# First block's queries and keys loaded in halves, four heads' bias tables behind them, matmuls over ones spread between the first quarters' scores

## The chip, the cores and the metric

The kernel runs on one core of a Trainium2 chip. The metric is device time in microseconds (us), taken over several executions; beside it one execution is recorded by the hardware profiler. The engines are named PE (TensorE; its weight loads are shown apart as PEld), DVE (VectorE), ACT (ScalarE), POOL (GpSimd) and SP (SyncE, which here only issues transfers).

## What is computed

Attention over 4 sequences of 576 tokens, 8 heads of 64, in a causal window of 128 with a linear position bias; a dense layer pair with h - tanh(h) between; and a layer of 8 experts in which each token goes to the one expert that fits it best.

```python
def _attn_ref(q, k, v):                      # 4 x 8 x 576 x 64 each
    scores = scale * np.matmul(q, k.transpose(0, 1, 3, 2))
    ...
    bias = slopes[:, None, None] * (-np.abs(rel).astype(np.float32))[None, :, :]
    mask = (rel >= 0) & (rel < window)       # window = 128
    scores = np.where(mask, scores + bias[None], -1000000000.0)
    attn = softmax(scores)
    return np.matmul(attn, v)

def _moe_ref(x, w_in, w_out):                # x 2304 x 512, w_in 512 x 2048
    h = x @ w_in
    return (h - np.tanh(h)) @ w_out

def _moe2_ref(x, expert_emb, tau, w1, w2):   # 8 experts of 512 x 1024 x 512
    logits = xn @ en.T / tau                 # of normalized rows
    expert_idx = np.argmax(logits, axis=1)
    ...
        out[mask] = gate_w[mask, None] * (np.maximum(x[mask] @ w1[e], 0.0) @ w2[e])
```

## The kernel before, in words

The 2304 tokens are 18 blocks of 128 rows, two blocks a group. A block's attention goes in four quarters of two heads each (function `quarter`): quarter number `a` is block `a // 4`, heads `2 * (a % 4)` and the next. For a quarter PE makes the scores (line 497 in the first four blocks, which work on plain float32 keys and queries), DVE adds the bias table and takes the maximum (line 525), ACT takes the exponentials (539), PE transposes them (560), ACT or DVE copies the transposes (564), and PE multiplies them with the values (574). Even quarters of the first two blocks write their scores to the bank "sc", odd ones to "acc". Per group, the rows are then transposed (678), multiplied with the weights of the dense layers (726, 750) and routed; the experts follow at the end.

The weights come as raw float32 and are split on the chip into a high and a low part: a load of 512 KB (line 347), a conversion on ACT or DVE (351), an assembly on DVE (354), the high part (359) and the low part (363). They are needed from about the third block on, so this work lies beside the attention of the first blocks.

Nothing of this is issued in the order of the source text. Every step is handed to a planner with `P.add(costs, function, due, r=..., w=...)`: which engines can do it and for how many us, when it is due, and which names it reads and writes. `Plan.order` takes, again and again, the step that can start first by these costs (the smaller due value where two can start at the same time), and so writes out one fixed order for each engine. SP's transfers share one assumed pipe in it. The order of all engines over the whole kernel comes from this one pass. The engines then run their queues in that order and wait for each other by semaphores.

At the start, `consts` loads the bias tables of the eight heads on ACT's queue, heads 0 and 1 first and heads 2 to 7 second, and then a mask `tri`, which the routing reads (line 876). SP loads queries and keys of the first block (`qk_early`, 256 KB each), a table of constants `con`, the values of the first block and then the other blocks' queries, keys and values and the raw weights. In the blocks 0 to 3 one transfer brings all eight heads of a block; its middle index is `hf * 2 + qq`, so the first two places are heads 0 to 3 (quarters 0 and 1) and the last two are heads 4 to 7.

`warm` puts matmuls over ones on PE, whose result nobody reads: `WARM[0]` of them at the very start, and `WARM[a + 1]` behind the scores of quarter `a`. Each is 128 x 128 by 512 columns in bf16. To the planner they read the bank of that quarter's scores, so that it places the softmax of the quarter behind them; on the chip they touch neither.

Of the kernel before, what the change touches and what calls it, by code (L numbers as in the profile page):

```python
# [23 lines left out]
B, H, S, D = 4, 8, 576, 64  # L24
# [23 lines left out]
WLEAD2 = 6  # L48
N0 = 1
NPX = 16  # L50
WARM = [7, 8, 2, 2, 2]
NALT = 8
NOWN = 8
NXO = 2
# [125 lines left out]
class Builder:  # L180
# [81 lines left out]

    def consts(self, P):
        nc, i = self.nc, self.i
        def table(e, h0, h1):
            nc.scalar.dma_start(out=self.bias[:, h0:h1, :],
                                in_=i["c_bias"][:, h0 * 256:h1 * 256].rearrange("p (h t) -> p h t", h=h1 - h0))

        for h0, h1 in ((0, 2), (2, H)):
            P.add({"AQ": 3.0}, lambda e, h0=h0, h1=h1: table(e, h0, h1), -40, w=[("bias", h) for h in range(h0, h1)])  # L270
        P.add({"AQ": 1.0}, lambda e: nc.scalar.dma_start(out=self.tri, in_=i["c_bias"][:, H * 256:]), -40, w=["tri"])

    def small(self):
        nc, i = self.nc, self.i
# [145 lines left out]
    def qk_early(self, P, b, due):  # L420

        nc, d2 = self.nc, b // 2

        def load_k(e):
            if b % 2 == 0:
                self.kf[d2] = self.wp.tile([128, 2, 4, 128], F32, tag=f"wo{FT - 1 - d2}", name=f"kf{d2}")
            nc.sync.dma_start(out=self.kf[d2][:, 1 - b % 2], in_=self.i["k0"][b])

        def load_q(e):
            if b % 2 == 0:  # L430
                self.qf[d2] = self.wp.tile([128, 2, 4, 128], F32, tag=f"w{'io'[d2]}{FT - 4}", name=f"qf{d2}")
            nc.sync.dma_start(out=self.qf[d2][:, b % 2], in_=self.i["q0"][b])

        both = lambda kind: [(kind, b)] + ([] if b % 2 else [(kind, b + 1)])
        P.add({"SP": 0.73}, load_q, -25 if b == 0 else due, r=["at"], w=both("qf"))
        P.add({"SP": 0.73}, load_k, -25 if b == 0 else due, r=["at"], w=both("kf"))

    def v_full(self, P, b, due):

# [29 lines left out]
    def quarter(self, P, a, due):  # L469

        nc = self.nc
        b, qd = divmod(a, 4)
        hf, qq = divmod(qd, 2)
        s, n = b % 2, (2 * b + hf) % 2
        one = b in NOPRE
# [8 lines left out]
        bank = "acc" if a < NALT and a % 2 else "sc"  # L484

        def scores(jj):
            sc = v["sc"][jj] = self.scores[jj] if bank == "sc" else self.psA.tile(
                [128, 2, 128], F32, tag=f"acc{jj}", name="scx", bufs=1)
            j = qq + 2 * jj
            hp, p0 = hf * 4 + j, 64 * jj  # L490
            if early:
                kt = [self.kf[x // 2][p0:p0 + 64, 1 - x % 2, hf * 2 + qq, :] for x in ([b] if one else [b, b - 1])]
                if b % 2 and not one:
                    kt = [self.kf[b // 2][p0:p0 + 64, :, hf * 2 + qq, :]]
                for m, k in enumerate(kt):
                    out = sc[:, 0:2, :] if b % 2 and not one else sc[:, m, :]
                    nc.tensor.matmul(out, lhsT=self.qf[b // 2][p0:p0 + 64, b % 2, hf * 2 + qq, :], rhs=k, start=True,  # L497
                                     stop=True)
                return
            q = self.qst[n]  # L500
            sl = s if one else slice(0, 2)
            for m in range(2):
                nc.tensor.matmul(sc[:, sl, :], lhsT=q[:, m, j, :], rhs=self.khl[:, sl, hp, :], start=(m == 0),  # L503
                                 stop=(m == 1))
# [118 lines left out]
        q = [("q", n), ("ql", n)]  # L623
        ttr = 0.4 if one else (0.52 if cs == 0 else 0.83)
        ttr += 0.13 * (2 * (b in SPLIT) + (b - 1 in SPLIT))
        for jj in range(2):
            if early:
                P.add({"PE": 0.3 if one else 0.42}, lambda e, jj=jj: scores(jj), due,
                      r=["at", ("qf", b)] + [("kf", x) for x in ([b] if one else [b, b - 1])], w=[(bank, jj)])
            else:  # L630
                P.add({"PE": 0.13 if one else 0.24}, lambda e, jj=jj: scores(jj), due,
                      r=["at"] + ks + [("kl", x, hf) for x in kv] + q, w=[(bank, jj)])
        if a + 1 < len(WARM) and WARM[a + 1]:
            self.warm(P, WARM[a + 1], -30, [(bank, 0), (bank, 1)])
        for jj in range(2):
            P.add({"DVE": ttr}, lambda e, jj=jj: soft(jj), due, r=["at", ("bias", qd * 2 + jj)],
                  w=[(bank, jj), ("mx", jj, a % 2)])
        for jj in range(2):
            P.add({"ACT": 0.49 if one else 0.64}, lambda e, jj=jj: exp(jj), due,
                  r=["at", (bank, jj), ("mx", jj, a % 2)], w=[("p32", pb, jj), ("sm", sk, qq, jj)])  # L640
        sm = [("sm", sk, x, y) for x in range(2) for y in range(2)]
        half = [("xr", 2 * hf), ("xr", 2 * hf + 1)]
        if early:
# [3 lines left out]
                  r=["at", ("tp", a)] + ([("h", own)] if own is not None else []), w=[("pt", a % 2)],  # L647
                  free="misc" if own is None else None)
            P.add({"PE": 0.45 if one else 0.9}, pv_f, due,
                  r=["at", ("pt", a % 2)] + [("vf", x) for x in ([b] if one else [b - 1, b])], w=[("o", qq)] if qq else ["o", ("o", 0), ("o", 1)])  # L650
            if qq:
# [4 lines left out]
              w=[("ph", a % 2)], port=True)  # L656
        P.add({"POOL": 0.84, "DVE": 0.46} if one else {"POOL": 1.19, "DVE": 0.71}, s_lo, due,
              r=["at", ("p32", pb, 0), ("p32", pb, 1), ("ph", a % 2)], w=[("ph", a % 2, 1)], port=True)
        P.add({"SP": 0.7 if one else 1.2}, tr, due, late=LATE, r=["at", ("ph", a % 2), ("ph", a % 2, 1)], w=[("pt", a % 2)])
        P.add({"PE": 0.28 if one else 0.56}, pv, due,  # L660
              r=["at", ("pt", a % 2)] + [("vt", x, hf, m) for x in kv for m in range(3)], w=["o"])
# [693 lines left out]
    def build(self):  # L1355
# [10 lines left out]
        P.add({"POOL": 2.7}, lambda e: self.small(), 0, w=["small", "cum"])  # L1366
        self.warm(P, WARM[0], -40)
        self.zero(P)
# [255 lines left out]
```

## Time and profile before

| | us |
|---|---|
| median of 3 runs | 773.45 |
| lowest and highest | 772.88, 774.47 |
| the profiled execution | 773.47 |
| its span, first to last instruction | 771.7 |
| busy in it: PE, DVE, ACT, POOL | 758.0, 548.5, 430.3, 306.1 |
| bytes moved by DMA | 124.62 MB |

The span starts with the first instruction and ends with the last; 1.77 us of the profiled execution lie outside it. A busy engine is one with an instruction in flight, and matmuls overlap each other, so the start of the next one says more on PE than the duration of one. Times of rows count from the span's start.

### The profile page before, as it was taken

The page shows a single profiled execution, that of the slowest core. Times are in us where ns is not written, and L with a number is a line of the kernel's source. Part 1 is how long each engine was busy: PE and PEld are TensorE (multiplying, and loading weights), DVE is VectorE, ACT ScalarE, POOL GpSimd, SP SyncE. Part 2 cuts the span into 40 slices and gives each one's busy share as a digit, 9 for nine tenths or more (in the row PEclk, how much of TensorE's full clock was granted, in tenths as well). Part 3 has the DMA queues.
Part 4 walks back from the last instruction along what each step waited for, and adds up shares of the span by engine and source line. Part 5 has one row for each costly group of instructions (what it writes and reads, how often), then busy time and mean ns, then how long its engine had stood idle before and what let it go on. Part 6 is the DMA issues. An engine that isn't in the chain of part 4 may idle for free.

```text
span 771.7 us, 15216 instructions
## 1 busy us (share of the span) xinstructions
PE 758.0 (98%) x5210; PEld 673.9 (87%) x5210; DVE 548.5 (71%) x1498; ACT 430.3 (56%) x971; POOL 306.1 (40%) x324
## 2 busy tenths in 40 slices
PE   8999999999999999999999999999999999999996
PEld 4878898798998999989899998998889989888895
DVE  4879898787777788778776776787627787677420
ACT  4878776565465555655654743656235564565321
POOL 0143335584665165364744732410103542531211
PEclk9999999999999999999999999999999999999999
DMA  9993749947554265464455252774268879896100
GB/s 348 401 361 111 210 132 300 212 121 142 141 114 131 61 124 119 101 125 129 98 121 124 65 82 74 180 229 148 89 169 209 223 229 252 209 245 226 44 29 31
DMA packets 152742, 124.62 MB, mean 161 GB/s; under 512 B 115461, under 2 KB 119557, under 8 KB 152400
## 3 DMA queue, kind: packets, MB, share of 16 engines
q1 hardware_dynamic: 149200, 111.19, 55.0%
q0 software_dynamic: 3024, 11.82, 4.2%
q8 instruction: 43, 0.70, 0.4%
q10 hardware_dynamic: 432, 0.56, 0.2%
q14 instruction: 43, 0.35, 0.1%
HBM read 84.65 MB, written 22.06 MB: 138 GB/s over the span
## 4 chain that ended last, share of the span: by engine, by line
PE 90%; issue 3%; DVE 3%; DMA 1%; ACT 1%; POOL 1%; SPq 0%; POOLq 0%; ACTq 0%; DVEq 0%
PE h L726 26%; PE acc L750 24%; PE he L1200 11%; PE y L1235 10%; PE o L585 4%; PE sc L503 3%; PE y L1231 3%; PE of L574 2%; PE sc L497 1%; PE misc L678 1%; PE misc L560 1%; PE ht L1320 1%; DMA est<-in_w 1%; PE misc L253 1%; PE misc L835 1%
## 5 line engine op out<-in xcount | busy, mean ns | idle before, releaser
L726 PE MATMUL h<-xT,wi 128*128 128x256 f32 x1728 | 225.7, 284 | 1.0 <-DVE t L734 1.0
L726 PEld LDWEIGHTS h<-xT,wi 128*128 128x128 f32 x1728 | 217.2, 191 | 6.4 <-DVE t L734 1.2
L750 PE MATMUL acc<-wo,gh 128*128 128x512 f32 x576 | 182.9, 398 | 0.6 <-DVE wo L363 0.5
L750 PEld LDWEIGHTS acc<-wo,gh 128*128 128x128 f32 x576 | 100.5, 189 | 16.9 <-DVE wo L363 1.2
L750 PE MATMUL acc<-wo,gl 128*128 128x512 f32 x288 | 112.7, 391 | 0.1
L731 ACT ACTIVATE t<-h 128x512 f32<-128x512 f32 x72 | 43.0, 598 | 107.8 <-PE h L726 100.4
L1235 PE MATMUL y<-eo,ge 128*128 128x512 f32 x336 | 88.0, 397 | 0.0
L539 ACT ACTIVATE p<-sc,mx 128x256 f32<-128x256 f32 (+1 forms) x128 | 58.8, 461 | 37.6 <-DVE mx L525 27.2
L549 POOL TENSOR_TENSOR ph<-p,ph 128x512 f16<-128x512 f32 (+1 forms) x39 | 45.8, 1175 | 60.4 <-ACT ph L544 44.9
L1235 PEld LDWEIGHTS y<-eo,ge 128*128 128x128 f32 x336 | 60.1, 188 | 10.1
L525 DVE CUSTOM_DVE_ANT_0 sc<-sc,bias 128x256 f32<-128x256 f32 (+1 forms) x136 | 49.3, 375 | 23.2 <-PE sc L503 14.2
L743 DVE TENSOR_TENSOR gl<-t,gh 128x512 fp32r<-128x512 f32 x72 | 61.6, 855 | 6.0 <-ACT gh L739 5.7
L1222 DVE SCALAR_TENSOR_TENSOR ge<-he,ge 128x256 fp32r<-128x256 f32 x104 | 28.8, 315 | 50.9 <-ACT ge L1216 50.4
L750 PEld LDWEIGHTS acc<-wo,gl 128*128 128x128 f32 x288 | 54.1, 188 | 12.5 <-DVE gl L743 0.4
L734 DVE TENSOR_TENSOR t<-h,t 128x512 f32<-128x512 f32 x72 | 49.4, 686 | 16.4 <-ACT t L731 16.2
L1216 ACT ACTIVATE ge<-he 128x288 fp32r<-128x288 f32 (+2 forms) x56 | 23.2, 414 | 64.7 <-PE he L1200 39.3
L1200 PEld LDWEIGHTS he<-xA,ei 128*128 128x128 f32 x384 | 54.2, 188 | 2.7
L1200 PE MATMUL he<-xA,ei 128*128 128x288 f32 (+2 forms) x384 | 55.9, 295 | 0.0
L1200 PEld LDWEIGHTS he<-xT,ei 128*128 128x128 f32 x384 | 53.5, 188 | 2.2
L1200 PE MATMUL he<-xT,ei 128*128 128x288 f32 (+2 forms) x384 | 54.9, 295 | 0.0
L397 POOL TENSOR_TENSOR khl<-stk,khl 64x512 fp32r<-64x512 f32 x25 | 33.9, 1356 | 52.8 <-ACT khl L393 50.6
L1098 DVE TENSOR_TENSOR eo<-est,eo 128x512 fp32r<-128x512 f32 x64 | 50.9, 795 | 5.2 <-ACT eo L1094 5.2
(221 smaller groups left out, 1339.9 us busy)
## 6 DMA issues: line engine op xcount, KB each, us to landing
est<-in_w SPq DMA_DIRECT2D x128, 256.0 KB, 3.6
bucket<-in_c_pad SPq DMA_DIRECT2D x8, 1155.0 KB, 9.8
rawi<-in_w_in SPq DMA_DIRECT2D x16, 511.8 KB, 8.1
rawo<-in_w_out SPq DMA_DIRECT2D x16, 511.8 KB, 8.9
stk<-in_k SPq DMA_DIRECT2D x30, 256.0 KB, 2.9
stq<-in_q SPq DMA_DIRECT2D x28, 256.0 KB, 3.0
vst<-in_v SPq DMA_DIRECT2D x30, 128.0 KB, 2.6
xe<-bucket SPq DMA_DIRECT2D x3, 384.0 KB, 3.5
```

The source lines that it names most:

```text
L397: self.eng(e).tensor_tensor(out=k, in0=r4("k")[64:128], in1=k.bitcast(F32), op=ALU.subtract)
L525: nc.vector.tensor_tensor_reduce(out=x, in0=x, in1=self.bias[:, h, c0:c1], scale=-0.125, scalar=mx[:, 1:2] if m else 3.0e38, op0=ALU.add, ...
L539: nc.scalar.activation(out=v["p32"][:, jj * W:(jj + 1) * W], in_=x, func=AF.Exp, scale=-1.0, bias=v["mx"][jj][:, 0:1], accum_out=self.sums ...
L549: self.eng(e).tensor_tensor(out=ph[:, 2 * W:4 * W], in0=v["p32"][:, 0:2 * W], in1=ph[:, 0:2 * W], op=ALU.subtract)
L726: nc.tensor.matmul(h3(v["h"], f2), lhsT=w[:, a, k, :], rhs=xT[c][:, :, k, :], start=(k == 0 and n == 0), stop=(k == KD - 1 and n == 2))
L731: nc.scalar.activation(out=v["t"], in_=v["h"].rearrange("p a b -> p (a b)"), func=AF.Tanh)
L734: nc.vector.tensor_tensor(out=v["t"], in0=v["h"].rearrange("p a b -> p (a b)"), in1=v["t"], op=ALU.subtract)
L743: self.eng(e).tensor_tensor(out=v["gl"], in0=v["t"], in1=v["gh"].bitcast(F32), op=ALU.subtract)
L750: nc.tensor.matmul(self.acc[g, t], lhsT=v[a][:, c0:c0 + 128], rhs=self.w["o", fs[f2]][:, c, :], start=(first and f2 == 0 and n == 0), stop ...
L1098: self.eng(eng).tensor_tensor(out=t[:, 1, :], in0=v["x"], in1=t[:, 0, :].bitcast(F32), op=ALU.subtract)
L1200: nc.tensor.matmul(h[:, 0:N], lhsT=w[:, a, c0:c0 + 128], rhs=xT()[b][:, k, 0:N], start=(k == 0 and n == 0), stop=(k == KD - 1 and n == 2))
L1235: nc.tensor.matmul(y[t], lhsT=gt(f, a)[:, (t - ts[0]) * 128:(t - ts[0] + 1) * 128], rhs=self.w["o", f0 + f][:, b, :], start=(f == 0 and n ...
```

## The change

`WARM` becomes 7, 2, 3, 2, 2 instead of 7, 8, 2, 2, 2. Queries and keys of block 0 come in two transfers each, heads 0 to 3 of both first, then heads 4 to 7 of both. The tables of heads 2 and 3 stay second on ACT's queue; those of heads 4 to 7 go to SP's queue behind `con`, and the mask `tri` goes to SP with a late due value. The scores of quarters 2 and 3 wait for the second halves.

```diff
-WARM = [7, 8, 2, 2, 2]
+WARM = [7, 2, 3, 2, 2]
...
     def consts(self, P):
         nc, i = self.nc, self.i
-        def table(e, h0, h1):
-            nc.scalar.dma_start(out=self.bias[:, h0:h1, :],
-                                in_=i["c_bias"][:, h0 * 256:h1 * 256].rearrange("p (h t) -> p h t", h=h1 - h0))
-
-        for h0, h1 in ((0, 2), (2, H)):
-            P.add({"AQ": 3.0}, lambda e, h0=h0, h1=h1: table(e, h0, h1), -40, w=[("bias", h) for h in range(h0, h1)])
-        P.add({"AQ": 1.0}, lambda e: nc.scalar.dma_start(out=self.tri, in_=i["c_bias"][:, H * 256:]), -40, w=["tri"])
+        def table(q, h0, h1):
+            q.dma_start(out=self.bias[:, h0:h1, :],
+                        in_=i["c_bias"][:, h0 * 256:h1 * 256].rearrange("p (h t) -> p h t", h=h1 - h0))
+
+        for h in (0, 2):
+            P.add({"AQ": 3.0}, lambda e, h=h: table(nc.scalar, h, h + 2), -40, w=[("bias", h), ("bias", h + 1)])
+        P.add({"SP": 0.73}, lambda e: table(nc.sync, 4, H), -18, w=[("bias", h) for h in range(4, H)])
+        P.add({"SP": 0.3}, lambda e: nc.sync.dma_start(out=self.tri, in_=i["c_bias"][:, H * 256:]), 8, w=["tri"])
...
-        def load_k(e):
-            if b % 2 == 0:
+        def load_k(e, m=None):
+            if b % 2 == 0 and not m:
                 self.kf[d2] = self.wp.tile([128, 2, 4, 128], F32, tag=f"wo{FT - 1 - d2}", name=f"kf{d2}")
-            nc.sync.dma_start(out=self.kf[d2][:, 1 - b % 2], in_=self.i["k0"][b])
+            c = slice(0, 4) if m is None else slice(2 * m, 2 * m + 2)
+            nc.sync.dma_start(out=self.kf[d2][:, 1 - b % 2, c], in_=self.i["k0"][b][:, c])
...
-        P.add({"SP": 0.73}, load_q, -25 if b == 0 else due, r=["at"], w=both("qf"))
-        P.add({"SP": 0.73}, load_k, -25 if b == 0 else due, r=["at"], w=both("kf"))
+        if b == 0:
+            for m in range(2):
+                P.add({"SP": 0.4}, lambda e, m=m: load_q(e, m), -25 + 5 * m, r=["at"], w=both("qf") if m == 0 else ["qf1"])
+                P.add({"SP": 0.4}, lambda e, m=m: load_k(e, m), -25 + 5 * m, r=["at"], w=both("kf") if m == 0 else ["kf1"])
+            return
+        P.add({"SP": 0.73}, load_q, due, r=["at"], w=both("qf"))
+        P.add({"SP": 0.73}, load_k, due, r=["at"], w=both("kf"))
...
-                      r=["at", ("qf", b)] + [("kf", x) for x in ([b] if one else [b, b - 1])], w=[(bank, jj)])
+                      r=["at", ("qf", b)] + [("kf", x) for x in ([b] if one else [b, b - 1])]
+                      + (["qf1", "kf1"] if b == 0 and hf else []), w=[(bank, jj)])
```

`load_q` is changed as `load_k` is.

## Rows read from the trace of the kernel before

**Rows 1.** The page: span, and busy time of each engine with its instructions.

```profile
span 771.7 us, 15216 instructions
PE 758.0 (98%) x5210; PEld 673.9 (87%) x5210; DVE 548.5 (71%) x1498; ACT 430.3 (56%) x971; POOL 306.1 (40%) x324
```

**Rows 2.** Chain of waits, first 16 us: start, us, what; pieces in order of time.

```profile
1.17 4.34 DMA kf<-in_k
...
5.65 0.80 PE sc L497 x4
6.44 3.53 PE misc L253 x8
9.97 0.73 PE scx L497 x4
10.70 0.54 PE misc L253 x2
11.24 0.41 PE sc L497 x2
11.65 0.37 PE misc L560 x2
12.02 0.42 PE sc L497 x2
12.44 0.54 PE misc L253 x2
12.97 0.45 PE of L574 x4
...
13.64 0.42 PE scx L497 x4
```

**Rows 3.** Timeline, merged: start, us, engine, line, what; in brackets idle time before it.

```profile
1.43 3.17 PE L253 MATMUL misc<-fill 128*128 128x512 bf16 x7 [1.43 <-DVE fill L257]
2.10 0.43 SPq L443 DMA_DIRECT2D vf<-in_v  x1
7.20 0.36 ACT L539 ACTIVATE p<-sc,mx 128x128 f32<-128x128 f32 x1
8.05 1.38 SPq L347 DMA_DIRECT2D rawi<-in_w_in  x3
13.82 0.77 ACT L351 CAST xrow<-rawi 128x512 f16<-128x512 bf16 x1
22.05 0.77 ACT L351 CAST x3T<-rawi 128x512 f16<-128x512 bf16 x1
```

**Rows 4.** Stretches: busy PE, PEld, DVE, ACT, POOL; granted clock, DMA share, GB/s.

```profile
6.44:9.97 3.53, 3.53 (x11) 1.05 (x10) 0.60 (x4) 0.81 (x4) 0.00 (x0) 1.00 1.05 387
20.00:50.00 30.00, 29.93 (x217) 25.18 (x216) 24.50 (x78) 24.41 (x63) 8.91 (x12) 1.00 1.02 402
60.00:74.20 14.20, 13.05 (x87) 11.23 (x85) 13.35 (x29) 12.27 (x25) 5.63 (x5) 1.00 0.40 129
137.00:154.10 17.10, 15.63 (x114) 12.97 (x114) 13.12 (x30) 10.27 (x25) 9.01 (x11) 1.00 1.04 224
```

**Rows 5.** Waits of PE over the span: waited for, us in total, times, longest.

```profile
PE misc L835 <- DVE xT L686: 1.4, 1, 1.4
```

**Rows 6.** DMA issues: queue, count, KB each, median us from issue to landing.

```profile
bias<-in_c_bias ACTq DMA_DIRECT2D x1, 128.0 KB, 3.3
vst<-in_v SPq DMA_DIRECT2D x30, 128.0 KB, 2.6
vf<-in_v SPq DMA_DIRECT2D x4, 256.0 KB, 4.6
rawi<-in_w_in SPq DMA_DIRECT2D x16, 511.8 KB, 8.1
bucket<-in_c_pad SPq DMA_DIRECT2D x8, 1155.0 KB, 9.8
```

**Rows 7.** Waits of SP's queue before 80 us, in the same columns as rows 5.

```profile
SPq L432 <- DMA bias<-in_c_bias: 1.0, 1, 1.0
```

More of the change, by code (lines that the diff above doesn't have):

```diff
@@ L422, in qk_early, with load_q @@
         nc, d2 = self.nc, b // 2
-        def load_k(e):
-            if b % 2 == 0:
+        def load_k(e, m=None):
+            if b % 2 == 0 and not m:
                 self.kf[d2] = self.wp.tile([128, 2, 4, 128], F32, tag=f"wo{FT - 1 - d2}", name=f"kf{d2}")
-            nc.sync.dma_start(out=self.kf[d2][:, 1 - b % 2], in_=self.i["k0"][b])
-        def load_q(e):
-            if b % 2 == 0:
+            c = slice(0, 4) if m is None else slice(2 * m, 2 * m + 2)
+            nc.sync.dma_start(out=self.kf[d2][:, 1 - b % 2, c], in_=self.i["k0"][b][:, c])
+        def load_q(e, m=None):
+            if b % 2 == 0 and not m:
                 self.qf[d2] = self.wp.tile([128, 2, 4, 128], F32, tag=f"w{'io'[d2]}{FT - 4}", name=f"qf{d2}")
-            nc.sync.dma_start(out=self.qf[d2][:, b % 2], in_=self.i["q0"][b])
+            c = slice(0, 4) if m is None else slice(2 * m, 2 * m + 2)
+            nc.sync.dma_start(out=self.qf[d2][:, b % 2, c], in_=self.i["q0"][b][:, c])
         both = lambda kind: [(kind, b)] + ([] if b % 2 else [(kind, b + 1)])
-        P.add({"SP": 0.73}, load_q, -25 if b == 0 else due, r=["at"], w=both("qf"))
-        P.add({"SP": 0.73}, load_k, -25 if b == 0 else due, r=["at"], w=both("kf"))
+        if b == 0:
[5 more added lines that the diff above has]
+        P.add({"SP": 0.73}, load_k, due, r=["at"], w=both("kf"))
     def v_full(self, P, b, due):
```

## Prediction

> **What bounds the kernel now.** The page comes first. TensorE (PE) is busy for 98% of a span of 771.7 us [rows 1], so a time is saved only where PE idles or where it does work that nothing needs. The chain of waits from the start is read next [rows 2]. From 1.17 to 5.51 us it is one transfer, the first block's keys, and PE starts the first scores at 5.65. The seven matmuls over ones that stand ahead end at 1.43 + 3.17 = 4.60 [rows 3], so PE idles 5.65 - 4.60 = 1.05 us. Then the chain lies on PE alone: scores of quarter 0, eight matmuls over ones (3.53 us), scores of quarter 1 (0.73), two more over ones, and so on up to the first product with the values at 12.97 (line 574).
>
> Nothing waited for those eight. Quarter 0's exponentials are done at 7.20 + 0.36 = 7.56 [rows 3], and their transposes stand in the chain only at 11.65, because PE's queue is in order.
>
> The durations also tell the clock. One matmul over ones takes 3.53 / 8 = 0.44 us in that stretch, 512 columns at about 1.2 GHz. Behind quarter 1's scores two take 0.54, and the four instructions of a first-block score pair fall from 0.73 to 0.42 (13.64) [rows 2]: that is the 2.4 GHz level. The granted clock of the slow stretch nevertheless reads 1.00 [rows 4], so here the level has to be read from durations. It rose near 10.70, after PE had been busy without a break from 5.65, and not during the seven matmuls before the pause.
>
> Behind that PE mostly stays the bound: 29.93 of 30 us busy from 20 to 50, and with its 98% of the whole span it has little idle time anywhere. Two stretches differ. From 60 to 74.2 VectorE (DVE) is busy 13.35 of 14.2 us, and from 137 to 154.1 PE is busy only 15.63 of 17.1 [rows 4], with one wait of 1.4 us for an xT made on DVE [rows 5].
>
> **The change part by part.**
>
> *Keys and queries in halves.* The transfers that quarters 0 and 1 need shrink from 256 KB to 128 KB each, and the second table DMA beside them from 384 to 128 KB. The half of the keys is SP's second issue as before, at 1.17. No row has it, so I bound it. Tiles of 128 KB in rows of the same 1 KB take 2.6 us in the median of 30 (vst), and the 128 KB table, which ran amid the same traffic, took 3.3 [rows 6]: the half lands between 3.8 and 4.5, or at worst at 5.51 as now. I take 4.4, by the table, since it is the nearest row. That is before 4.60, so the pause of 1.05 us goes.
>
> *The Trainium skill has a rule against this part.* In "Perfetto Trace Analysis", section "DMA Optimizations", it says that small DMAs under 2 KB have significant overhead per transfer, and a half brings rows of 1 KB. By it the pause would stay. The 2.6 and 3.3 us of [rows 6] are for rows of 1 KB and speak the other way.
>
> *Fewer matmuls over ones.* Eight become two behind quarter 0, two become three behind quarter 1. I rebuild the chain [rows 2] from 4.60 with its own pieces. Scores 0.80 give 5.40, two matmuls over ones at 0.44 give 6.28, scores of quarter 1 with 0.73 give 7.01. For what follows the clock decides. I let it rise at the same place of the program, behind quarter 1's scores: by then PE has been busy without a break since 1.43. Then three matmuls at 0.27 give 7.82, and the same four pieces as now (0.41 + 0.37 + 0.42 + 0.54 = 1.74) give 9.56 instead of 12.97: **3.41 us saved**. The ends: at the fast level from the first scores on, the sum is 4.60 + 0.42 + 0.54 + 0.42 + 0.81 + 1.74 = 8.53, 4.4 us saved. With the slow level until 10.70 as now, and every piece until then at twice its fast price, it is 7.01 + 1.32 + 0.82 + 0.74 + 0.84 + 0.54 = 11.27, 1.7 us saved. I take 3.4.
>
> *What the chain must find ready.* Scores of quarter 0 ending at 5.40 give exponentials 1.1 us later as now (6.44 to 7.56), at 6.5; the transposes are due at 7.82 + 0.41 = 8.2. The values of block 0 are now fourth on SP and become ninth. SP holds a later issue until an early transfer has landed (1.0 us on the bias, [rows 7]), and some 0.5 MB more goes ahead of them: at 387 GB/s [rows 4] 1.3 us more than their issue at 2.10 [rows 3] plus 4.6 [rows 6], so about 8.0 against a need at 9.56. The cover is some 1.6 us; beyond it each us is lost.
>
> *Tables and mask.* The tables of heads 4 to 7 move from ACT's queue to SP's, sixth, behind con. There they go ahead of the values, and so land before the 8.0 just estimated, by three transfers of 262 KB each (2.0 us at 387 GB/s) at about 6; quarter 2's softmax needs them after 8.2. The mask tri goes to SP among the late weights; its first reader is a matmul of the routing (line 876), behind the first groups. Three issues more at about 0.43 us each lie on SP at the start; SP is not in the chain there except through its first two issues. All this costs nothing as long as these covers hold.
>
> *How much arrives at the end.* PE is full from 12.97 to 50, so its work there starts and ends 3.4 us sooner if its inputs do. Of these the loads don't move. The first raw weight, is converted at 13.82, the second, issued at 8.05, only at 22.05 [rows 3]. A load of that kind takes about 8 us [rows 6], so from the second on there are 6 us of slack or more, and the first alone is tight. From 60 to 74 DVE is the bound, but it idled 5.5 of the 30 us before 50 [rows 4], more than 3.4, so it can start its run sooner. I carry the 3.4 through in full.
>
> The profiled execution took 773.47 us, 1.77 over its span; the median of the runs is 773.45. 773.47 - 3.4 = **770.1 us**.
>
> **The rivals.**
>
> *The halves land no sooner.* For it: they share the engines with two tables and their own successors. Against it: [rows 6]. The pause stays, the rest holds: 3.41 - 1.05 = 2.4, so 771.1.
>
> *The clock stays low longer.* PE's filler falls from 21 matmuls to 16. For it: seven in a row left PE at the slow level before the pause. Against it: the scores and transposes fill the gaps, and PE has no pause left. If it rises no sooner than now, 1.7 us remain: 771.8. The Trainium skill bears on this one ("TensorE: Matmul & The Clock Gate", "What's actually happening": the default state is throttled, and activity releases the throttle). By that rule, less filler could cost what this rival costs; the durations of [rows 2] show the release, but not which activity was needed.
>
> *The first raw weight catches ScalarE (ACT).* It converts the weight at 13.82 without waiting, and its exponentials queue behind that. Moved 3.4 us forward it would come at 10.4, and a weight that lands as late as 13.8 takes the whole 3.4 back: 773.5. Against it: the planner counts the load's landing when it places the conversion, and by its costs two loads of 256 KB now go behind this weight instead of ahead (2 x 0.262 MB / 387 GB/s = 1.35 us sooner). About a third of the gain left, 772.3.
>
> *The new order collides later, and the time ends slower.* The planner orders all 771 us anew from the changed first entries. The place is 137 to 154, where PE already runs dry. The transposes of the probabilities leave SP there between writes of c_pad of 1155 KB, 9.8 us to landing [rows 6], with the DMA engines full (1.04 at 224 GB/s, [rows 4]). One such write that comes ahead of a transpose there costs 1.18 MB / 224 GB/s = 5.3 us, which nothing hides since PE has no other work left. Then 773.5 - 3.4 + 5.3 = 775.4. It decides from 3.4 us of such delay on. Against it: the steps there are tied to each other and would all shift together.
>
> **How the numbers follow.** Forecast 0.52 (770.1, own range 768.8 to 771.5: the clock's ends and small shifts of the order), halves no sooner 0.10 (771.1), clock low 0.09 (771.8), first weight 0.16 (772.3), collision 0.13 (775.4). What a measurement can tell from no change is 0.2%, 1.55 us, so faster means below 771.9. The forecast, the halves and half of the clock's case lie there: 0.52 + 0.10 + 0.04 = 0.66. Slower is the collision, 0.13; the rest, 0.21, is the same. The range leaves out the collision and about 0.05 below 768.0, where the fast clock and a better order would meet: 768.0 to 773.4.
>
> **What would show it.** The first scores start at 4.6 or before 4.7 with no pause ahead of them; two matmuls over ones behind quarter 1 at 0.27 each, not 0.44; line 574 first near 9.6; the first exponentials of quarter 2 not held by a table; the first raw weight's conversion with no idle time of ACT before it. Then the same places later each some 3.4 us sooner: the end of the DVE run at 74.2, the wait for xT at 154.1, the end. The prediction is wrong if the front saves 3 us and 154.1 doesn't move by as much, or if the first product with values waits for vf.

## The result: slower, and the profile after

The changed kernel takes 780.56 us in the median of 6 runs (779.47 to 785.30), the kernel before 773.43 (772.88 to 775.18): a ratio of 1.0101, interval 1.0081 to 1.0121. I had said 770.1 and 768.0 to 773.4. The profiled executions are 779.47 against 773.47 us, so 6.0 us later.

The page of the changed kernel, span and busy time, answers to [rows 1]. TensorE (PE) has five matmuls fewer and yet is busy 1.2 us longer, and its idle time grew from 13.7 to 18.4 us.

```profile
span 777.6 us, 15216 instructions
PE 759.2 (98%) x5205; PEld 675.4 (87%) x5205; DVE 548.2 (71%) x1497; ACT 430.4 (55%) x973; POOL 304.3 (39%) x323
```

The front came close to what was forecast. PE's timeline of the changed kernel (start, us, line, what, idle time before it), for [rows 2]:

```profile
4.53 0.80 PE L505 MATMUL sc<-kf,qf 64*128 64x128 f32 x4
5.26 1.03 PE L253 MATMUL misc<-fill 128*128 128x512 bf16 x2
6.22 0.80 PE L505 MATMUL scx<-kf,qf 64*128 64x128 f32 x4
6.95 1.02 PE L253 MATMUL misc<-fill 128*128 128x512 bf16 x3
...
9.97 0.68 PE L582 MATMUL of<-vf,ptf 128*128 128x128 f32 x4 [0.26 <-ACT p32x L547]
```

The pause for the keys is gone (4.53 where 5.65 stood), and the first product with values starts at 9.97. The same view of the kernel before:

```profile
12.81 0.61 PE L574 MATMUL of<-vf,ptf 128*128 128x128 f32 x4
```

So the two executions are 2.8 us apart there. How much of this is the change, and how much the clock of the two executions, is told behind the table of leads. ScalarE's (ACT's) cast of the first raw weight comes at 13.71 without a wait.

The loss comes later. The waits of PE from 30 to 90 us in the changed kernel (waited for, us in total, times, longest); the kernel before has two there, 1.0 and 0.5 us:

```profile
PE acc L759 <- DVE wo L364: 3.3, 2, 3.2
PE h L735 <- DVE t L743: 1.4, 2, 0.8
PE h L735 <- ACT wi L360: 1.2, 1, 1.2
...
PE h L735 <- DVE wi L364: 0.4, 1, 0.4
```

L360 and L364 split a weight into its two parts, the second on VectorE (DVE). Three of the six rows of this view, 3.3 + 1.2 + 0.4 = 4.9 us, are waits for a weight to be split. Stretches of the changed kernel (as in [rows 4]):

```profile
60.00:62.00 2.00, 0.72 (x3) 0.52 (x4) 1.97 (x6) 2.00 (x6) 0.90 (x2) 1.00 0.99 373
62.00:65.00 3.00, 3.00 (x13) 2.81 (x13) 2.62 (x3) 1.44 (x4) 1.52 (x1) 0.50 0.37 119
65.00:66.00 1.00, 1.00 (x4) 0.78 (x4) 0.51 (x1) 1.00 (x2) 0.96 (x1) 0.79 0.86 227
...
70.00:75.00 5.00, 1.85 (x13) 1.35 (x11) 4.64 (x13) 3.64 (x9) 2.83 (x2) 1.00 0.61 143
50.00:100.00 50.00, 43.10 (x286) 37.96 (x286) 44.61 (x101) 39.88 (x85) 21.26 (x20) 0.97 0.50 160
```

And of the kernel before:

```profile
70.00:75.00 5.00, 3.97 (x33) 3.76 (x33) 4.90 (x9) 4.49 (x9) 0.10 (x1) 1.00 0.08 28
50.00:100.00 50.00, 48.25 (x328) 42.82 (x327) 44.94 (x94) 41.36 (x84) 15.62 (x14) 1.00 0.61 192
```

Between 50 and 100 us PE works 48.25 - 43.10 = 5.15 us less. After it had stood idle for 1.28 of the 2 us from 60 to 62, the granted clock was 0.50 for 3 us and 0.79 for one, 3 x 0.5 + 0.21 = 1.7 us more. Together 6.9 us, against 2.8 saved at the front and a span 5.9 us longer: these two account for 4.1 of the 5.9; of the other 1.8 us, 0.6 are idle time of PE from 30 to 50 us (busy 19.30 us there, 19.93 before); the rest I have not found in one place.

The same stretch seen through the line of the weights' split alone (stretch, its length, DVE's busy time and count on that line, then granted clock, DMA share, GB/s), before:

```profile
55.00:75.00 20.00, 6.56 (x10) 1.00 0.45 144
```

and in the changed kernel:

```profile
55.00:75.00 20.00, 3.64 (x6) 0.91 0.70 213
```

Six weights are split there instead of ten. What DVE and ACT did in that time is attention: the first transposes of block 4's probabilities leave SP at 66.24 us, where the kernel before sends them at 78.47. Nothing in the diff asks for that. The planner orders all work by its own list of costs and due times, and with other entries at the front it gave another order for what follows.

### The profile page after: what moved, and what is told of

It reads as the page before. It is cut to its first block, busy times and chain, and to the rows that moved or that the text cites. A ratio compares the mean times of both kernels' runs of the same rounds, so it can differ in the third digit from the quotient of the medians.

```text
span 777.6 us, 15216 instructions
## 1 busy us (share of the span) xinstructions
PE 759.2 (98%) x5205; PEld 675.4 (87%) x5205; DVE 548.2 (71%) x1497; ACT 430.4 (55%) x973; POOL 304.3 (39%) x323
## 4 chain that ended last, share of the span: by engine, by line
PE 76%; issue 2%; DMA 1%; ACT 0%; POOL 0%; DVE 0%; POOLq 0%; ACTq 0%
PE h L735 21%; PE acc L759 20%; PE he L1209 12%; PE y L1244 11%; PE o L593 3%; PE y L1240 3%; PE sc L511 3%; DMA pt<-ph 1%; PE ht L1329 1%; PE misc L687 1%; PE misc L844 1%; POOL out L1269 0%; PE misc L1132 0%; PE misc L858 0%; ACT yo L1265 0%
## 5 line engine op out<-in xcount | busy, mean ns | idle before, releaser
L557 POOL TENSOR_TENSOR ph<-p,ph 128x512 f16<-128x512 f32 (+1 forms) x37 | 44.0, 1190 | 54.7 <-ACT ph L552 36.5
L752 DVE TENSOR_TENSOR gl<-t,gh 128x512 fp32r<-128x512 f32 x72 | 59.5, 826 | 6.1 <-ACT gh L748 5.5
L1159 POOL TENSOR_TENSOR xf<-xe 128x512 f32<-128x512 bf16 (+2 forms) x19 | 21.1, 1113 | 80.5 <-DVE xT L1169 28.7
```

The lines of the kernel that those rows point to most:

```text
L557: self.eng(e).tensor_tensor(out=ph[:, 2 * W:4 * W], in0=v["p32"][:, 0:2 * W], in1=ph[:, 0:2 * W], op=ALU.subtract)
L752: self.eng(e).tensor_tensor(out=v["gl"], in0=v["t"], in1=v["gh"].bitcast(F32), op=ALU.subtract)
```

## Whose loss is it: the order's, or the edits'?

**Theory**: the new order, by its late weights. **Rival**: the edits themselves (small transfers, missing matmuls over ones). A planned task may issue other instructions than it was planned with, so front and order can be exchanged.

**1. The new front in the order of before.** Planned as before, issued with two and three matmuls over ones; the halves and tables are issued by the tasks that loaded the whole ones, in the changed kernel's sequence.

```diff
+PUT = [7, 2, 3, 2, 2]                      # issued; WARM = [7, 8, 2, 2, 2] is planned
...
-            for _ in range(n):
+            for _ in range(put or n):
```

> This kernel has the change's work at the start (halves, tables of heads 4 to 7 on SP, 7, 2, 3, 2, 2 matmuls over ones; the mask goes to SP behind the expert embeddings), but the planner is given the costs and names of before, so that every engine keeps the order of before. Theory 'order' (the 3 us saved at the front are real, and the planner's new order of the rest throws away more): the front's saving comes through, 770.2 us (769 to 771.5), first product with values near 10, no PE wait of 3 us for a weight between 60 and 80. Theory 'bound' (VectorE's and ScalarE's splitting of the weights bounds the first 100 us, so that an earlier TensorE finds nothing ready): the saving is waited away by 75 us, 773 to 774. Theory 'direct' (the new transfers themselves delay what follows): slower than before, 777 to 781.

Measured: 776.15 us (773.42 to 777.72), ratio 1.0025 [1.0005, 1.0044]. So 4.4 of the 7.1 us are gone with the order, but the front's gain has not come either: the median lies 3.0 us above that of the kernel before, measured beside it (773.17), and none of the three theories has the number. ACT, and PE behind it:

```profile
13.56 0.76 ACT L359 CAST xrow<-rawi 128x512 f16<-128x512 bf16 x1 [3.23 <-DMA rawi<-in_w_in]
14.69 0.70 PE L513 MATMUL scx<-kf,qf 64*128 64x256 f32 x2 [2.40 <-ACT p32x L555]
```

That is my rival of the first raw weight, at nearly its full size. The rest of it is told with runs 5 to 12.

**2. The old front in the new order.** Planned as the changed kernel, issued with whole loads and eight and two matmuls over ones.

```diff
+PUT = [7, 8, 2, 2, 2]                      # WARM = [7, 2, 3, 2, 2] is planned
...
-            c = slice(0, 4) if m is None else slice(2 * m, 2 * m + 2)
+            if m == 1:
+                return
+            c = slice(0, 4)
```

> The reverse: the work at the start is that of before (whole queries and keys, tables on ACT's queue, 7, 8, 2, 2, 2 matmuls over ones), but the planner is given the costs and names of the changed kernel, so that every engine has the changed kernel's order. Theory 'order': as slow as the changed kernel or slower by up to the 3 us of the front, 780 to 784 us, with the TensorE wait for a weight's low part near 73 in the trace. Theories 'bound' and 'direct': about as before, 773 to 774.

Measured: 782.71 us (781.16 to 783.77), ratio 1.0113 [1.0083, 1.0142], with the same waits as the changed kernel:

```profile
PE acc L769 <- DVE wo L370: 3.4, 2, 3.3
PE h L745 <- DVE t L753: 1.4, 2, 0.8
PE h L745 <- ACT wi L366: 1.2, 1, 1.2
```

The order alone costs 782.71 - 773.17 (before, same batch) = 9.5 us. The new front gives back 782.71 - 780.56 = 2.2: in the two traces the first h matmul stands at 30.52 and 28.54, and the routing's product behind its wait for xT at 162.92 and 160.98, so the front's 2.0 us are carried through 130 us unchanged (run 2 ran its eight matmuls over ones at the low level, in 3.41 us).

**3 and 4. Each half of the change with its own order.** First only `WARM = [7, 2, 3, 2, 2]`, then only the loads and tables.

> Only the counts of matmuls over ones change (7, 2, 3, 2, 2), with the loads of before, planned anew. The pause of 1.05 us stays. Theory 'order': the planner's order is new here too, and on its own clock the 16th weight's low part comes 2.5 us later than in the order of before (10.6 us later in the changed kernel's), so a part of the loss shows: 773 to 777. Theory 'direct': the loads are those of before, so 2.4 us faster, 771.

Measured: 780.48 us (778.45 to 785.09), ratio 1.0086 [1.0056, 1.0115].

> Only the loads change (halves, tables and mask on SP), with 7, 8, 2, 2, 2 matmuls over ones, planned anew. Theory 'order': on the planner's own clock the 16th weight's low part comes 3.5 us later than in the order of before; 774 to 778, whatever the front does (1 us saved there). Theory 'direct': the whole loss is here, 778 to 781 or more.

Measured: 782.45 us (781.14 to 784.38), ratio 1.0118 [1.0087, 1.0150]. Either half alone loses as much as both. Run 3 is slower than either side had it, and run 4 by its number lies on the side of 'direct'. What speaks against 'direct' are runs 9 and 10 below: the same halves of the change, in the order of before, take 774.88 and 774.95 us. The waits of runs 3 and 4 sit at other places (3.0 us for ACT's p in the first, 2.7 us for DVE's t in the second): two more orders, both bad.

**5. Another order with nothing else changed.**

```diff
-        P.add({"PE": 0.22 * n}, run, due, r=[("gh", 0), *r], w=[("h", 0)])
+        P.add({"PE": 0.221 * n}, run, due, r=[("gh", 0), *r], w=[("h", 0)])
```

> Same work, loads and number of matmuls over ones as before; only the planner's price of one matmul over ones is 0.221 instead of 0.22, which gives another order from about 40 us on. On the planner's own clock the 16th weight is split at 76.7, against 71.5 for the kernel before and 82.1 for the changed one. Theory (an order that splits the weights later starves TensorE between 50 and 90 us): between the two, about 778 us (776 to 781), with TensorE waiting for weights between 55 and 90 us. Rival (the loss comes from the moved loads or the missing matmuls over ones themselves, the order is neutral): 772.5 to 774.

Measured: 780.22 us (779.26 to 782.42), ratio 1.0077 [1.0048, 1.0107], as the theory had it. Waits of PE, 30 to 90 us:

```profile
PE h L726 <- DVE t L734: 2.9, 2, 2.2
PE h L726 <- DVE wi L363: 1.6, 1, 1.6
PE h L726 <- DVE xT L686: 0.8, 1, 0.8
```

A thousandth of a microsecond in the planned cost of a matmul over ones is worth 780.22 - 773.81 = 6.4 us, with the same work. By its page four instructions have moved from POOL (324 to 320) to ACT and DVE (971 to 974, 1498 to 1499): the planner also chooses the engine of a step, and "order" stands for both here. Runs 2 to 5 are four orders other than that of before, and they cost 6.4 to 9.5 us: **the order is what lost the time**. Only 1.6 us of these waits are for a weight; late weights are one form of it.

**6. Weights first.** The changed kernel, with block 4's late scores made to follow the split of one weight in the planner.

```diff
-                      r=["at"] + ks + [("kl", x, hf) for x in kv] + q, w=[(bank, jj)])
+                      r=["at"] + ks + [("kl", x, hf) for x in kv] + q + ([(("i", 5), 1)] if b == NF else []), w=[(bank, jj)])
```

> The changed kernel, all its loads and matmuls over ones kept, with one more dependency in the planner alone: the late scores of block 4 are placed after the split of the sixth weight of the first product. The planner then splits the 16th weight at 73.6 on its clock instead of 82.1. Theory (late weights are the loss): the waits for weights between 55 and 90 us shrink to under 2.5 us together, and the time is 771 to 775 us, 5 to 9 below the changed kernel. Rival (the order costs by something other than the weights): 778 us or more, with the weights split early all the same.

Measured: 779.95 us (777.75 to 783.08), ratio 1.0070 [1.0045, 1.0094]. Nine weights are split from 55 to 75 us, and the waits for them fall to 1.6 us, as the theory had it; but the time is the rival's. The trace:

```profile
50.00:100.00 50.00, 46.08 (x312) 40.94 (x311) 43.83 (x86) 37.89 (x73) 13.28 (x12) 1.00 0.37 130
155.00:160.00 5.00, 2.66 (x26) 2.11 (x26) 2.30 (x7) 2.47 (x7) 4.84 (x6) 0.84 0.90 183
160.00:165.00 5.00, 5.00 (x39) 4.96 (x40) 2.18 (x11) 1.56 (x5) 0.60 (x1) 0.82 0.44 109
```

From 50 to 100 us PE regains 46.08 - 43.10 = 3.0 of the 5.15 us. From 155 to 165 it loses much of that again: 2.34 us idle, 1.66 of them for a transpose of probabilities on its way through the DMA queue (the kernel before stands 1.4 near there, for an xT, [rows 5]), and 5 x 0.16 + 5 x 0.18 = 1.7 us to the clock. So the late weights are where the changed kernel stood, but mending that place alone doesn't make its order a good one.

## Where the front's gain goes when the order stays

The runs 7 to 12 (and 1) all keep the order of before, so the same instruction can be compared. The table takes four marks from PE's timeline: the first product with values, the first h matmul, the router's product behind the wait of 1.4 us for xT [rows 5], and the end of the span; in brackets how far ahead of before.

| kernel | first product with values | first h | router's product behind the xT wait | span |
|---|---|---|---|---|
| before | 12.81 | 32.59 | 154.09 | 771.7 |
| 1: new front | 9.21 (3.60) | 31.54 (1.05) | 153.01 (1.08) | 773.9 (-2.2) |
| 7: raw weight earlier | 8.83 (3.98) | 31.52 (1.07) | 153.54 (0.55) | 772.8 (-1.1) |
| 8: cast later | 8.86 (3.95) | 31.00 (1.59) | 153.07 (1.02) | 770.7 (1.0) |
| 9: fewer ones only | 9.16 (3.65) | 32.52 (0.07) | 154.01 (0.08) | 774.2 (-2.5) |
| 10: loads only | 9.53 (3.28) | 32.87 (-0.28) | 154.36 (-0.27) | 773.1 (-1.4) |
| 11: 8, attention's loads sooner | 9.03 (3.78) | 29.76 (2.83) | 151.22 (2.87) | 768.7 (3.0) |
| 12: fewer ones, loads sooner | 12.54 (0.27) | 33.90 (-1.31) | 155.38 (-1.29) | 773.4 (-1.7) |

Two things are read from it. From the first h to 154 us every lead is kept within 0.6 us, through the stretch where DVE is full [rows 4]. And of a lead of 3.3 to 4.0 us at the first product with values, runs 1, 7, 8, 9 and 10 have 1.6 us or less left by 32. What eats it?

One caution comes first: these leads are counted from a single execution of the kernel before, in which the clock rose late. Run 5 is the measure for that. Up to 36 us its PE, ACT, DVE and SP do the same steps in the same order as the kernel before, with its loads and its eight matmuls over ones. PE there:

```profile
5.95 1.90 PE L253 MATMUL misc<-fill 128*128 128x512 bf16 x8
...
10.38 0.61 PE L574 MATMUL of<-vf,ptf 128*128 128x128 f32 x4
...
30.16 1.67 PE L726 MATMUL h<-xT,wi 128*128 128x256 f32 x12
```

The eight end with the next scores at 7.78, so they took 1.83 us, the 2.4 GHz level, where the kernel before paid 3.53 at the 1.2 GHz level [rows 2]. With nothing changed at the front, run 5 is 12.81 - 10.38 = 2.43 us ahead at the first product with values and 32.59 - 30.16 = 2.43 at the first h. So up to 2.4 us of a lead in the table can be the clock of the execution. Counted from run 5, the front of runs 1 and 7 to 11 is ahead by 0.85 to 1.55 us at the first product, and at the first h only run 11 is ahead, by 0.40. Which wait takes a lead back can still be read from each trace; how many microseconds the change itself gives cannot be read from the brackets.

**7. The first raw weight's load issued right behind the first values**, four loads earlier.

```diff
         def load(e):
             ...
+        if j == 0:
+            self.load0, load = load, lambda e: None
...
             self.nc.sync.dma_start(out=self.vf[b // 2][:, b % 2, :], in_=self.i["v"][b * 128:(b + 1) * 128, :])
+            if b == 0:
+                self.load0(e)
```

> The new front in the old order, as in the first experiment, with the first raw weight's load issued right behind the first values, four loads earlier. Theory (in the old order ScalarE, which works in order, stood 3.23 us for that load and TensorE 2.40 us behind it): the wait goes, the lead over the kernel before at 31 us grows from 1.07 to about 3.2 us, and the time is 776.15 - 2.4 = 773.7 if the clock falls at 152 us again, 770 to 772 if it doesn't. Rival (the loads pushed back by it stop the quarters of blocks 1 and 2 instead): a new wait of 1 to 2.5 us at 9 to 16 us, and 774.5 to 776.5.

Measured: 774.36 us (772.28 to 778.82), ratio 1.0007 [0.9984, 1.0029]. PE's wait at 14 us is gone, but the lead at 31 us is 1.07 as it was, not 3.2. Two new waits have come. The first is the rival's, a little shorter than it said: PE stands 0.91 us for block 1's keys, one of the loads pushed back.

```profile
12.18 0.70 PE L518 MATMUL sc<-kf,qf 64*128 64x256 f32 x4 [0.91 <-DMA kf<-in_k]
```

The second comes at 27 us. ACT and PE there:

```profile
26.01 0.62 ACT L404 CAST khl<-stk 128x512 fp32r<-128x512 f32 x1 [2.86 <-DMA stk<-in_k]
27.14 0.71 PE L518 MATMUL sc<-kf,qf 64*128 64x128 f32 x4 [1.78 <-ACT p32x L560]
```

**8. ACT's cast of that weight issued later**, just ahead of DVE's step on it; the loads as in run 1.

> The new front in the old order with the loads as in the first experiment; ScalarE's cast of the first raw weight is issued later, just ahead of VectorE's step on that weight, so that the exponentials of the next quarters stand ahead of it in ScalarE's queue. Theory (the cast's place in the queue is what stopped the softmax): TensorE's wait of 2.40 us at 12 to 15 us goes, the same lead of about 3.2 us at 31 us as with the earlier load, 770 to 774 us. Rival (the late transfer itself is what counts, the weight is needed that soon): the wait moves to VectorE's step on the weight and the lead stays near 1 us, 775 to 777 us.

Measured: 774.22 us (771.82 to 778.11), ratio 1.0006 [0.9985, 1.0026]. Neither side is right: the wait at 14 us goes and the lead is 1.59 us, not 3.2 and not 1. ACT stands for the first late keys instead:

```profile
25.49 0.62 ACT L406 CAST khl<-stk 128x512 fp32r<-128x512 f32 x1 [2.42 <-DMA stk<-in_k]
26.62 0.71 PE L518 MATMUL sc<-kf,qf 64*128 64x128 f32 x4 [1.23 <-ACT p32x L560]
```

In the kernel before, the timeline and the DMA issues of the first 16 us (median us to landing) have that load so:

```profile
14.99 0.33 SPq L387 DMA_DIRECT2D stk<-in_k  x1
...
25.96 0.62 ACT L393 CAST khl<-stk 128x512 fp32r<-128x512 f32 x1
```

```profile
stk<-in_k SPq DMA_DIRECT2D x1, 256.0 KB, 9.0
```

Issued at 14.99, landed 9.0 us later at 24.0, read at 25.96: 2.0 us of slack, when PE, ACT and DVE were all to arrive 3 us sooner.

**9 and 10. Each half of the change alone, in the order of before.**

> One part alone, in the order of before: two and three matmuls over ones instead of eight and two, all loads as before. TensorE's front is 2.4 us shorter, the pause for the keys stays. Theory (the transfers set the first 50 us: the loads' slack before their readers in the kernel before is about 0.5 us for the first raw weight and 1.94 us for the first late keys, so no more than that can be carried): ScalarE waits 1.5 to 2.2 us for the first raw weight, TensorE is 0.3 to 1.2 us ahead of before at 32 to 46 us, and the time is 772.5 to 774 us. Rival (only the added small transfers of the new front hold it back): no wait for the raw weight over 0.7 us, a lead of 2 us and more, 771 us.

Measured: 774.88 us (771.12 to 779.37), ratio 1.0011 [0.9987, 1.0034]. With every load as before, the first raw weight still stops ACT, longer than expected; less of the lead is left, and the time is 0.9 us above the theory's range. The cast, and two stretches behind it (as [rows 4]):

```profile
12.97 0.76 ACT L352 CAST xrow<-rawi 128x512 f16<-128x512 bf16 x1 [2.70 <-DMA rawi<-in_w_in]
```

```profile
14.00:17.00 3.00, 2.90 (x12) 1.71 (x12) 0.73 (x4) 2.43 (x11) 0.00 (x0) 0.69 1.02 412
17.00:20.00 3.00, 3.00 (x19) 2.42 (x18) 2.46 (x11) 1.72 (x5) 0.00 (x0) 0.74 1.03 411
```

The kernel before reads that weight at 13.82 [rows 3] without a wait; here it is there at 12.97, and in run 5, with the same loads, its cast starts at 12.12 behind a wait of 0.62 us. So its slack was about 0.9 to 1.7 us, and not much beyond that can be gained while the cast keeps its place. In this execution PE was 12.81 - 9.16 = 3.65 us ahead at the first product with values, lost 1.87 behind ACT and 3 x 0.31 + 3 x 0.26 = 1.7 to the clock that fell after that wait: 0.08 is left, as the table has it.

> The other part alone, in the order of before: keys and queries in halves and the tables and the mask behind them, with eight and two matmuls over ones as before. TensorE starts the scores 1.1 us sooner. Theory (the halves and tables move fewer bytes per us at 4 to 6.4 us, so every later load lands about 1 us later): the first raw weight comes late for ScalarE, which waits about 1 us; 10.5 to 10.8 MB moved by 30 us against 11.0, TensorE within 0.7 us of before at 32 to 46 us, and the time 773 to 775 us. Rival (the transfers catch up, the gain of 1.1 us is carried): 771.8 to 772.5 us.

Measured: 774.95 us (773.50 to 777.73), ratio 1.0022 [1.0004, 1.0041], as the theory had it; the wait is 2.69 us where I expected one. All eight matmuls over ones are still there, yet the first product with values comes 3.28 us sooner (table): the eight took 1.83 us here too, so only about 1.1 of it is the pause. The DMA rows of the first 30 us (rate, packets, MB, mean rate), before and then this run:

```profile
GB/s 0 0 74 246 411 410 372 361 388 393 391 380 391 404 377 391 409 418 420 404 398 399 396 423 426 377 426 426 369 418 412 390 409 415 388 393 399 401 396 366
DMA packets 4390, 11.00 MB, mean 367 GB/s; under 512 B 612, under 2 KB 868, under 8 KB 4387
```

```profile
GB/s 0 0 55 320 348 319 192 290 355 333 317 306 363 410 407 434 393 415 426 404 420 404 388 410 415 404 404 431 393 407 388 434 377 409 393 409 404 399 366 407
DMA packets 4672, 10.61 MB, mean 354 GB/s; under 512 B 645, under 2 KB 1541, under 8 KB 4669
```

Each figure of the rate is a slice of 0.75 us. From 3.75 to 9 us it is 192 to 355 where the kernel before has 361 to 410; behind that both run at about 400. By 30 us 0.39 MB are missing, about 0.39 MB / 402 GB/s [rows 4] = 1.0 us of transfers by which later loads lie back (run 9, with the loads of before, had moved 10.89 MB). The Trainium skill has this effect ("Perfetto Trace Analysis", "DMA Optimizations": significant overhead per transfer under 2 KB). The trace agrees, if a packet is taken for the page's transfer: the count under 2 KB went from 868 to 1541 as the rate fell. How much of it is the 1 KB rows and how much the tables' new place was not tried apart.

**11. Attention's loads sooner.** Run 8, and each load of late keys, queries and values of the first 60 us moved on SP ahead of up to four raw weights, as far as its buffer is free.

```diff
...
+            if e == "SP" and self.times[at][0] < 60.0 and (".qk_half." in name(n) or ".v_half." in name(n)):
+                deps, to, left = self.tasks[n][3], at, k
+                while left and to and seq[to - 1][0] not in deps:
+                    to -= 1
+                    if seq[to][1] == "SP" and ".weight." in name(seq[to][0]):
+                        left, best = left - 1, to
+                if left < k:
+                    seq.insert(best, seq.pop(at))
...
```

> The new front in the old order with ScalarE's first cast later, as in the run before, and each load of late keys, queries and values of the first 60 us issued up to four raw weights earlier on SP. Theory (these loads have 1.6 to 2 us of slack in the kernel before and the weights 4 to 18, so it is their place in the queue that takes back the front's gain): ScalarE's waits for stk and vst before 50 us shrink from 4.8 to under 1 us, the lead over before at 45 us grows from 1.4 to between 2.6 and 3.4 us, and the time is 769.5 to 771.5 us. Rival (in 15 to 50 us something else stands right behind them, the weights or VectorE): the lead stays under 1.8 us, 772.5 to 774 us.

Measured: 772.20 us (770.50 to 773.62), ratio 0.9981 [0.9964, 0.9999] to 773.15; the profiled execution is 770.50. The lead is what the theory had, the profiled time too; the median is 0.7 us above its range. The late keys are read at 23.25 without a wait, and the sequence stands 2.9 us sooner up to the end (page, then timeline):

```profile
span 768.7 us, 15211 instructions
```

```profile
23.25 0.64 ACT L425 CAST khl<-stk 128x512 fp32r<-128x512 f32 x1
...
151.22 0.45 PE L875 MATMUL misc<-en,x3T 128*128 128x24 bf16 x12 [1.40 <-DVE xT L726]
```

Runs 8 and 11 differ in these loads alone, and their fronts are alike (3.95 and 3.78 us ahead at the first product with values). From there to the first h, run 8 loses 2.36 us of its lead and run 11 0.95. So **the place of these loads in the queue is what took back much of the lead; with them moved, 2.8 of 3.8 us are left at 30 us, and stay to the end of this execution**. Not shown is that all of it is gained by the change, since run 5 had 2.4 us at the same place by its clock alone. This is the one kernel whose interval lies below 1, though in the medians by 0.95 us only; its own runs lie at 770.5 to 771.0 (five) and 772.1 to 773.6 (seven).

**12. Without the halves.** Fewer ones, loads whole, cast later, attention's loads sooner.

> Fewer matmuls over ones in the old order, keys and queries whole and the tables as before, ScalarE's first cast later and the late keys, queries and values up to four raw weights sooner on SP. Theory: without the halves the front gives 2.4 us instead of 3.4, but no load lands later; all of it is carried, TensorE is 2.0 to 2.4 us ahead at 45 us, and the time is 770.5 to 772 us. Rival (as in the run before): a lead under 1.3 us, 772.5 to 774 us.

Measured: 773.51 us (770.05 to 778.15), ratio 0.9996 [0.9976, 1.0017]: inconclusive. The profiled execution (775.16) was behind from the start, by the clock:

```profile
8.26 1.46 PE L273 MATMUL misc<-fill 128*128 128x512 bf16 x3
...
14.35 0.60 PE L273 MATMUL misc<-fill 128*128 128x512 bf16 x2
```

By row length over count, a matmul over ones takes 1.46 / 3 = 0.49 us at 8.3, the 1.2 GHz level, and 0.60 / 2 = 0.30 at 14.4, the 2.4 GHz level. In run 9, the same front, that stretch was already fast (three in 0.82). No wait for a load is left in its trace before 30 us but that for the keys; what it would give with an early clock stays open, though its fastest run, 770.05, is the fastest of all twelve kernels.

## Why the prediction was wrong

**The front was right in most parts, and partly by luck.** The halves came in time (scores at 4.53 for 4.60, the pause gone), and no table held anything up. 2.8 us were saved at the first product with values for 3.41 forecast. The mis-sized terms, from start to start: the two and the three matmuls over ones took 0.96 us each (5.26 to 6.22, 6.95 to 7.91) where I took 0.88 and 0.81, and 0.26 us of wait were added. That wait shows that the cover of 1.6 us for the values wasn't there. The trace puts it down to ACT, but the values, issued at 4.54, landed only 5.3 us later, at 9.84, for a product at 9.97; I had them at 8.0. In run 6, with the same loads and an earlier clock, PE stands for them:

```profile
9.72 0.68 PE L582 MATMUL of<-vf,ptf 128*128 128x128 f32 x4 [1.15 <-DMA vf<-in_v]
```

So in the changed kernel the values were nearly in time only because the clock rose late: that was luck.

**The 3.41 rests on the clock of one execution.** I took the 3.53 us of the eight matmuls over ones as their price. Run 5 pays 1.83 for the same eight. My rival on the clock asked how late it rises in the new kernel, and never how late it had risen in the trace of before. With an early rise (by about 6 us) on both sides the front is worth 0.85 us by its loads (run 10), 1.22 by fewer ones (run 9) and 1.2 to 1.6 by both (runs 1, 7, 8, 11), each against run 5 at the first product with values. No run shows which rise is the usual one.

**"I carry the 3.4 through in full" failed, for a reason in front of it.** I treated the rest of the program as a fixed sequence that shifts. It is planned anew, and runs 2 to 5 show new orders that cost 6.4 to 9.5 us, whichever edit causes them. My rival "the new order collides later" had the kind right and the place wrong: not the transposes among c_pad's writes at 137 to 154 (only run 6 stands there, 1.66 us) but weights and attention competing for DVE at 50 to 90 us, the stretch that I had read as DVE's [rows 4] and used only to ask whether DVE could start sooner. Its 0.13 was the real mistake. I had argued that "the steps there are tied to each other and would all shift together", which no row showed; and with PE idle for 13.7 us of 771.7 [rows 1] there was little left for an order to win and much to lose.

**In the order of before the sentence would have failed too.** My slack was counted for the raw weights only ("from the second on there are 6 us of slack or more, and the first alone is tight"). The first was tight, about 0.9 to 1.7 us (runs 9, 5). "6 us or more" was read from the second weight alone: the first of the second layer's weights (rawo), issued at 10.12 in the kernel before, landed 9.4 us later at 19.5 and was cast at 23.36, and in run 8 it landed at 20.1 and was cast at 20.37. The loads that I left out are those of the late keys, with 2.0 us; they lie in the same transfer queue. I had the row for it: DMA share 1.02 from 20 to 50 us [rows 4] says that transfers are as full as PE there. Run 11 moves them, and 2.8 of its 3.8 us are left at 30 us and to the end. That DVE's run from 60 to 74 lets the lead through, as I had said, is right.

**The price of small transfers** I weighed only against the pause, where there was none (4.53). It lies in the rate: 0.39 MB fewer by 30 us (run 10), which my sum had at zero.

**The clock rival** (0.09) was not a case beside the others. Runs 9 and 12 issue the same loads and matmuls over ones at the front, and their first product with values stands at 9.16 and 12.54; 0.45 of these 3.38 us are later keys (scores at 5.38 and 5.83), the rest goes with the clock.

## What to carry to other kernels

Where a planner or a greedy scheduler orders the work, an edit at the front is two changes, the edit and a new order; price the order by perturbing it (the same work, one cost changed by a trifle), or keep the old order and exchange only what is issued. Before carrying a gain on, list for every load on the path, not just the largest, when it lands and when it is read: here a lead was cut down at each load whose slack was smaller than it. Before a gain at the start is read from two traces, compare the duration of the same instructions in both; here one front differed by 2.4 us from one execution to another. If transfers and TensorE are both full, move the loads in the same edit.

## What was not expected of the hardware

The granted clock's fall is not set by the idle time alone. The wait of 1.4 us at 154 us is in every kernel with the order of before. In that kernel, in 7, 8, 11 and 12 the clock stayed at 1.00 behind it, in 1, 9 and 10 it fell. The stretch in run 1 (as [rows 4]), and in before:

```profile
153.00:157.00 4.00, 3.98 (x33) 3.86 (x33) 2.57 (x8) 1.75 (x6) 2.89 (x3) 0.57 0.91 233
```

```profile
153.00:157.00 4.00, 2.91 (x37) 2.87 (x37) 2.98 (x8) 2.26 (x7) 3.94 (x4) 1.00 0.69 152
```

4 x 0.43 = 1.7 us for one such fall, more than the wait itself. Medians a microsecond apart, as those of before and run 11, therefore hold such falls as well as the work.

The rise varies as well: the same eight matmuls over ones took 3.53 us in the kernel before and 1.83 in run 5, and the granted clock in the rows reads 1.00 in both. The Trainium skill says of the rise that its point varies with the phase in which the first matmul arrives ("TensorE: Matmul & The Clock Gate", "What's actually happening"); the traces agree that it varies, and none of them shows the phase.

A late place varies too: the waits of PE for the outputs' evacuation near 660 to 680 us are 0.2 us in the kernel before and 1.4 and 1.6 in runs 1 and 7. In run 7 that is most of the 1.65 us by which its span falls behind its lead at 154; in run 1 it is 1.2 of 3.3 us, and the clock's fall 1.7.
